# Routing attention with a PReLU layer: two pairs of batch 0 transposed by VectorE, a third pair of batch 2 in cluster order, GpSimd's transfers without pace tokens

## The chip, the cores and the metric

The kernel runs on one core of one Trainium2 chip. The time is device microseconds (us) of that core, the median of several runs of the whole kernel. The profile comes from one further execution. A core has five engines, each with its own instruction queue that is worked off in order: TensorE (PE; its weight loads are PEld), VectorE (DVE), ScalarE (ACT), GpSimd (POOL) and SyncE (SP), which here only issues transfers (DMA). Engines wait for each other through semaphores.

## The reference, cut to what matters

```python
# batch 4, heads 8, tokens 768, head size 64, clusters 16
q_assign = argmax(q_n @ c_n.T);  k_assign = argmax(k_n @ c_n.T)   # per token and head
mask   = q_assign[:, :, :, None] == k_assign[:, :, None, :]
scores = where(mask, scale * q @ k.T, -1e9)
attn   = softmax(scores);  attn_out = attn @ v
x = attn_out.transpose(0, 2, 1, 3).reshape(3072, 512)
h = x @ w_in                                      # 512 -> 2048
out = (maximum(h, 0) + alpha * minimum(h, 0)) @ w_out   # 2048 -> 512
```

A query attends only to keys of its own cluster. The weights come in 64-bit floats and are converted on the chip; everything is computed in 32-bit floats.

## The kernel before, in words

**Units of work.** Two heads make a pair; batch b has pairs 4b to 4b+3 (`pairs`, 16 in all). A step is two of the six key chunks of a pair. An ordinary pair is done in two halves of 384 queries, each in three steps: scores (`score`, L781), exponential on ScalarE (L802), masking by cluster on VectorE (`mask`, L822), sums of the rows (L832, L870, L878), weighing of v (`weigh`, L936) and normalisation into xT (`normalise`, L1039). PSUM has one tile for the weighed values (`vps`), so the next pair's weighing waits for the normalisation of the one before. In batch 0 the mask is added to the scores by a matmul (L790) of cluster memberships (`member`, `outside`, `aq`), and sums are taken by a matmul with ones (L929).

**Pairs in cluster order.** From pair `NO` = 10 on (the last two pairs of batch 2, all of batch 3) tokens are first sorted by cluster: GpSimd scatters q, k and v rows to DRAM (`order_scatter`, L673; twelve rows of tiles to each head, staged by SyncE in `order_stage`, L659), and the sorted pair is loaded again (`order_load`). A key chunk then needs only a window of 224, 320 or 384 queries, not all 768 (`window`, `weigh_near`, L969), and the pair takes three steps rather than six. Its result is turned to rows by TensorE (`to_rows`, L999), scattered back by GpSimd (`put_back`, L1008), fetched by SyncE and turned by VectorE (`fetch_back`, `turn_back`, L1027).

**The order.** `steps` lists the steps: batch 0 and 1 have 24 each, then batch 2's cluster-ordered pairs come before its ordinary ones, then batch 3; `NS` = 78. The order of the instructions on each engine is written out by hand: load and preparation pieces are hung on a step and a slot (`load_at`, `prep_at`), others come due a number of slots later (`later`, `tick`). Matmuls of the layer (`ffn_pieces`: 28 pieces to a half batch, L1063 and L1081) fill the slots evenly from one entry of `begun_at` to the next; `kept` says how many are left for the block after. The very last half batches use a scheme with fewer products (`last_pieces`).

**The first half of batch 0** (steps 0 to 11) also converts weights. SyncE loads a raw tile of 512 KB (L247; five tiles in rotation), VectorE splits it (L253, L255), ScalarE scales, VectorE joins (L265, L268), GpSimd multiplies (L271). The number of conversions begun in steps 0 to 11 is 2, 0, 2, 2, 0, 2 and then one each. All of it stands at fixed places in VectorE's queue. Batch 0's pairs are loaded in one transfer a tile (`load`, L119); TensorE transposes them by an identity (`prep_features`, L354, three groups of eight matmuls a pair) and ScalarE copies them out (L358). For later batches the load places 32x32 blocks (L127), and VectorE transposes (`prep_blocks`, L364).

**Pace.** `pace` has ScalarE write a token (L649) and GpSimd copy it (L650), so that GpSimd's next transfer waits until ScalarE has come to that slot.

**Semaphores of transfers.** Transfers of SyncE and ScalarE share eight completion semaphores in the program's order; a transfer waits until the one that used its semaphore before has landed.

Of the kernel before, what the change touches and what calls it, by code (L numbers as in the profile page):

```python
# [10 lines left out]
FP32 = mybir.dt.float32  # L11
# [3 lines left out]
I32 = mybir.dt.int32  # L15
# [8 lines left out]
def kernel(  # L24
# [77 lines left out]


    pairs = [(b, hp) for b in range(B) for hp in range(NCH)]
    NO = WHOLE * NCH - 2
    NP = len(pairs)
    raw_qk, vts = {}, {}

    Q = 32

    def load(n):

        b, hp = pairs[n]
        for w, src in enumerate((q, k)):
            raw = inp.tile([P, 2, NJ, D], FP32, name="qk")
            if n < NCH:
                nc.sync.dma_start(  # L119
                    out=raw.rearrange("p h j d -> p h (j d)"),  # L120
                    in_=src[b, 2 * hp:2 * hp + 2].rearrange("h (p j) d -> p h (j d)",
                                                            j=NJ))
            for h in range(2):
                rows = src[b, 2 * hp + h]
                for x in range(D // Q if n >= NCH else 0):
                    r = h * D + x * Q
                    nc.sync.dma_start(  # L127
                        out=raw.rearrange("p h j d -> p (h j d)")[r:r + Q, :].rearrange(
                            "p (t i) -> p t i", i=Q),
                        in_=rows[:, x * Q:(x + 1) * Q].rearrange("(t p) i -> p t i", p=Q))  # L130
            raw_qk[n, w] = raw
# [192 lines left out]
    lowest = const.tile([P, B], FP32, name="lowest")  # L324
    highest = const.tile([P, B], FP32, name="highest")
    WORDS = [float((127 + e) * 2 ** 23) for e in (-50, 40)]
    kept_of = [0]

    def inverse(n, half):

        if pairs[n][0] > kept_of[0]:
            check_inverses()
        return inverses[:, (2 * n + half) % (2 * NCH), :]

    def check_inverses():
# [156 lines left out]
    def second_part():  # L492

        first_part.close()
        for name, bufs in (("emore", 1), ("ordc", 1), ("ordp", 1), ("order", NP - NO),
                           ("xmore", 1), ("byrow", 1), ("pace", 8)):
            sorts[name] = fast.enter_context(tc.tile_pool(name=name, bufs=bufs))
        for i in range(5):
            e_tiles.insert(0, sorts["emore"].tile([P, 2, HS], FP32, name=f"more{i}"))

    def order_constants():
# [21 lines left out]
        same = brief[:, 2 * P:3 * P]  # L523
        before, within = rows[1], rows[2]
        shift = ordc.tile([P, 2], FP32, name="shift")
        sorts["paced"] = ordc.tile([1, 1], FP32, name="paced")

        def columns():
            nc.vector.tensor_reduce(out=cols, in_=own, axis=AX.X, op=ALU.add)
# [113 lines left out]
            nc.vector.tensor_reduce(out=first, in_=begunT, axis=AX.X, op=ALU.add)  # L643
        firsts[n] = first

    def pace():

        token = sorts["pace"].tile([1, 1], FP32, name="pace")
        nc.scalar.copy(token, ones[0:1, 0:1])  # L649
        nc.gpsimd.tensor_copy(out=sorts["paced"], in_=token)  # L650

    def order_stage(n, i):

        b, hp = pairs[n]
# [24 lines left out]
    def order_load(n):  # L679
        assert len(scattered[n]) == 2 * NX  # L680
        whole = scratch.pop(n)[0]
        found = sorts["order"].tile([P, 2, NJ, 1], I32, name="found")
        for h in range(2):
            r0 = 2 * h * S
            nc.sync.dma_start(out=found[:, h], in_=whole.bitcast(I32)[
                r0:r0 + S, D:D + 1].rearrange("(j p) d -> p j d", p=P))
        orders[n] = found
        for w in range(2):
            raw = inp.tile([P, 2, NJ, D], FP32, name="qk")
            for h in range(2):  # L690
                r0 = (2 * h + w) * S
                for x in range(D // Q):
                    r = h * D + x * Q
                    nc.sync.dma_start(
                        out=raw.rearrange("p h j d -> p (h j d)")[r:r + Q, :].rearrange(
                            "p (t i) -> p t i", i=Q),
                        in_=whole[r0:r0 + S, x * Q:(x + 1) * Q].rearrange(
                            "(t p) i -> p t i", p=Q))
            raw_qk[n, w] = raw
        vt = vpool.tile([P, 2, NJ, D], FP32, name="vt")  # L700
        for h in range(2):
            r0 = (2 * h + 1) * S
            nc.sync.dma_start(out=vt[:, h], in_=whole[r0:r0 + S, D:2 * D].rearrange(
                "(j p) d -> p j d", p=P))
        vts[n] = vt
# [20 lines left out]
    for b in range(B):  # L726
        whole = [n for n in range(b * NCH, (b + 1) * NCH) if n >= NO]
        rest = [n for n in range(b * NCH, (b + 1) * NCH) if n < NO]
        begun_at.append(len(steps))
        steps += [(n, None, s) for n in whole for s in range(SB)]  # L730
        for half in range(2) if rest else ():
            if half:
                begun_at.append(len(steps))
            steps += [(n, half, s) for n in rest for s in range(SB)]
            feeds[len(steps)] = b, half
    begun_at.append(len(steps))
    assert NJ == 6 and GROUP == 2

# [265 lines left out]

    def put_back(to, place, rows, i):
        j, h = divmod(i, 2)
        pace()
        nc.gpsimd.indirect_dma_start(  # L1008
            out=to[i],
            out_offset=bass.IndirectOffsetOnAxis(ap=place[:, h, j:j + 1], axis=0),  # L1010
            in_=rows[j // HJ][:, j % HJ, h * D:(h + 1) * D], in_offset=None, element_offset=h * S * D)

    def fetch_back(n, whole):
# [11 lines left out]
        def turn_back():  # L1025
            for half in range(2):
                nc.vector.transpose(out=x_tile(b, half)[:, hp, :],  # L1027
                                    in_=raw[:, half * HS:(half + 1) * HS])
        later(4 if n == NP - 1 else 9, turn_back)

    def x_tile(b, half):
        if (b, half) not in xTs:
# [106 lines left out]
    def last_pieces():  # L1139
# [93 lines left out]
        def hidden(x):  # L1233
# [33 lines left out]

            def p3():
                plus(g_of(f1, 1), product("e", "S4", x_of(1, 1), False))
                slopes(f1)  # L1270

            def p7():
                plus(g_of(f2, 1), product("a", "S3", x_of(1, 0), False))
                late.append(p4)
                if x % 2 == 0 and x:
                    g_sums(x - 2)
# [86 lines left out]
    FREE = SLOTS * SB - 3  # L1363


    ORDERS = [26, 29, 35, 38, 41, 50]
    prep_at, load_at = {}, {}
    for (n, half), u in start_of.items():
        def at(step, slot, piece):
            prep_at.setdefault((step, slot), []).append(piece)  # L1370
        if half is None:
            t = ORDERS[n - NO]
            load_at.setdefault(t, []).append(lambda n=n: load(n))
            for i in range(2):
                at(t + 1, FIRST + i, lambda n=n, i=i: order_features(n, i))
            at(t + 2, 2, lambda n=n: order_sims(n))
            load_at.setdefault(u - (3 if n == NO + 1 else 4), []).append(
                lambda n=n: order_load(n))
            at(u - 4, 0, lambda n=n: prep_clusters(n))
            for i in range(2):  # L1380
# [3 lines left out]
        if half == 0:  # L1384
# [5 lines left out]
            else:  # L1390
                load_at.setdefault(u - 9, []).append(lambda n=n: load(n))
                load_at.setdefault(u - 7, []).append(lambda n=n: load_v(n))
            if n < NCH:
                for g in range(len(groups)):
                    at(u - 4, FIRST + g, lambda n=n, g=g: prep_features(n, g))
            else:
                for w in range(2):
                    at(u - 7, FIRST + w, lambda n=n, w=w: prep_blocks(n, w))
            at(u - (3 if n < NCH else 5 if u - 6 < TOGETHER else 6), FIRST,
               lambda n=n: prep_sims(n))  # L1400
            if n >= NCH:
                at(u - 4, FIRST if u - 4 < TOGETHER else 0, lambda n=n: prep_clusters(n))
        if n < NCH:
# [19 lines left out]
    def feed_block(u):  # L1423
        if u == NS:
# [2 lines left out]
                ffn[i] = lambda piece=ffn[i], p=p: (piece(), w_in_sums(p))  # L1427
            ffn.extend(last_pieces())
            return
        ffn.extend(ffn_pieces(*feeds[u]))  # L1430

    def kept(u):


        return {NS: 12, begun_at[-2]: 8, begun_at[-3]: 2}.get(block_end(u), 0)

    def block_end(u):
        return min(x for x in begun_at if x > u)
# [59 lines left out]
    for u in range(TOGETHER, NS + 1):  # L1498
# [54 lines left out]
        for i in slots:  # L1553
# [4 lines left out]
            places = (block_end(u) - block_start(u)) // SB * FREE  # L1558
            pieces = len(ffn) - kept(u) + -whole * (places - 1 - at_slot) // places
            todo.popleft()()  # L1560
            room = 0 if steps[u - SB][1] is None else 1 + (s == 0)
            if room and sorting:
                pace()
            while sorting and room:
                scatters, piece = sorting.popleft()
                piece()
# [229 lines left out]
```

## Time and profile before

| | |
|---|---|
| median of 3 runs | 945.04 us (944.75 to 946.84) |
| the profiled execution | 944.23 us, span 942.5 us |
| TensorE clock granted | 0.999 |
| busy: PE, PEld | 924.1, 496.5 us |
| busy: DVE, ACT, POOL | 663.5, 265.9, 351.2 us |
| chain that ended last | PE 87%, DVE 6%, SP's queue 2%, DMA 2% |
| transfers of SP and ACT | 60.35 MB in 201840 packets on the large queue |

Batch 0's first half runs from 13.5 to about 74 us, its second half to 196, batch 1 to 445, batch 2 to 644, batch 3 to about 750, and the last half batches of the layer to the end. A group in the profile is given as line, engine, operation, tile written <- tiles read, size and count, then busy time and mean duration in ns of one record, then the idle time of the engine just before them and what ended it. A float32 matmul leaves two records. Busy time of overlapping records counts once.

### The profile page before, as it was taken

The numbers are of one execution on the slowest core, as the hardware profiler recorded it, in microseconds if no ns is written. First come the engines' busy times: TensorE is split into PE (matmuls) and PEld (weight loads), VectorE is DVE, ScalarE is ACT, GpSimd is POOL, SyncE is SP. The second block draws the span as 40 slices with busy tenths as digits, with TensorE's granted clock in tenths as the row PEclk, the third lists the DMA queues.
The fourth block names the chain that finished last, engine by engine and source line by source line (L and its number), as shares of the span: only waits on it lengthen the run. The fifth ranks groups of instructions, "written<-read, shape, count | busy, mean of one in ns | idle before, by whom it ended". The sixth has DMA issues, their size and how long they took to land.

```text
span 942.5 us, 11891 instructions
## 1 busy us (share of the span) xinstructions
PE 924.1 (98%) x3995; PEld 496.5 (53%) x3995; DVE 663.5 (70%) x1247; ACT 265.9 (28%) x658; POOL 351.2 (37%) x529
## 2 busy tenths in 40 slices
PE   8999999999999999999999999999999999999997
PEld 5534444445455454454544545545455555556886
DVE  5797788799679589698995955456888535698100
ACT  5764444323123032331322322223133121221000
POOL 2333222200016576467534686364256670000000
PEclk9999999999999999999999999999999999999999
DMA  8333658039001645165920134333441112000000
GB/s 297 125 127 96 146 130 149 18 59 198 1 6 53 159 87 133 47 120 131 155 52 12 43 80 101 63 67 62 93 75 34 32 37 53 1 0 1 23 23 26
DMA packets 209668, 73.38 MB, mean 78 GB/s; under 512 B 194288, under 2 KB 198080, under 8 KB 209600
## 3 DMA queue, kind: packets, MB, share of 16 engines
q1 hardware_dynamic: 201840, 60.35, 29.2%
q0 software_dynamic: 6912, 11.81, 4.1%
q8 instruction: 33, 0.54, 0.2%
q10 hardware_dynamic: 848, 0.39, 0.2%
q14 instruction: 35, 0.29, 0.1%
HBM read 49.89 MB, written 22.28 MB: 77 GB/s over the span
## 4 chain that ended last, share of the span: by engine, by line
PE 87%; DVE 6%; SPq 2%; DMA 2%; issue 1%; POOL 1%; ACT 1%; ACTq 0%; DVEq 0%; POOLq 0%
PE fps L1081 26%; PE fps L1063 25%; PE vps L936 7%; PE sps L781 7%; PE sps L1297 4%; PE sps L1241 4%; PE fps L781 2%; PE vps L1297 2%; PE vps L1241 2%; PE fps L1297 1%; PE fps L1241 1%; PE sps L790 1%; PE vps L969 1%; PE mps L969 1%; PE mps L381 1%
## 5 line engine op out<-in xcount | busy, mean ns | idle before, releaser
L1063 PE MATMUL fps<-xT,w_in_sb 128*128 128x384 f32 x768 | 257.7, 490 | 0.0
L1081 PE MATMUL fps<-w_out_sb,gT 128*128 128x512 f32 x576 | 254.4, 595 | 1.1 <-DVE gT L1055 1.1
L1063 PEld LDWEIGHTS fps<-xT,w_in_sb 128*128 128x128 f32 x768 | 142.8, 190 | 102.6 <-issue 3.8
L1081 PEld LDWEIGHTS fps<-w_out_sb,gT 128*128 128x128 f32 x576 | 107.5, 190 | 133.4 <-issue 123.0
L673 POOL DMA_INDIRECT scratch<-stage,off x144 | 155.4, 1079 | 49.7 <-issue 25.1
L650 POOL COPY paced<-pace 1x1 f32<-1x1 f32 x196 | 55.5, 283 | 202.3 <-ACT pace L649 201.5
L1069 ACT COPY gT<-fps 128x384 f32<-128x384 f32 x96 | 46.0, 479 | 215.6 <-PE fps L1063 215.6
L1055 DVE SCALAR_TENSOR_TENSOR gT<-gT,alpha 128x384 f32<-128x384 f32 x96 | 61.3, 648 | 50.4 <-ACT gT L1069 50.3
L781 PE MATMUL sps<-qkT 64*128 64x384 f32 (+1 forms) x480 | 88.6, 487 | 0.0
L1008 POOL DMA_INDIRECT back<-rows,found x72 | 74.9, 1040 | 18.2 <-issue 16.1
L802 ACT ACTIVATE E<-sps 128x768 f32<-128x768 f32 (+1 forms) x78 | 57.9, 790 | 59.4 <-PE sps L790 38.8
L781 PEld LDWEIGHTS sps<-qkT 64*128 64x128 f32 x480 | 42.7, 186 | 40.5 <-issue 15.0
L822 DVE SCALAR_TENSOR_TENSOR more<-aq,key,more 128x384 f32<-128x384 bf16 (+2 forms) x120 | 63.0, 584 | 1.2 <-ACT more L799 1.1
L936 PE MATMUL vps<-E,vt 128*64 128x384 f32 x316 | 58.6, 495 | 1.4 <-DVE xT L1039 1.4
L904 DVE RECIPROCAL inverses<-mps 64x12 f32<-64x12 f32 (+1 forms) x44 | 10.9, 248 | 58.5 <-PE mps L891 58.1
L822 DVE SCALAR_TENSOR_TENSOR E<-aq,key,E 128x384 f32<-128x384 bf16 (+2 forms) x96 | 50.2, 577 | 1.9 <-ACT E L799 1.8
L271 POOL TENSOR_TENSOR w_in_sb<-w_in_sb,power 128x512 f32<-128x512 f32 x16 | 25.1, 1573 | 67.8 <-DVE w_in_sb L268 67.8
L832 DVE TENSOR_TENSOR acc<-acc,E 128x768 f32<-128x768 f32 x37 | 35.3, 953 | 14.7 <-ACT E L802 13.6
L271 POOL TENSOR_TENSOR w_out_sb<-w_out_sb,power 128x512 f32<-128x512 f32 x16 | 22.9, 1434 | 57.3 <-DVE w_out_sb L268 57.3
L802 ACT ACTIVATE more<-sps 128x768 f32<-128x768 f32 (+1 forms) x42 | 31.1, 775 | 33.1 <-PE sps L781 32.0
L1087 ACT COPY y<-fps 128x512 f32<-128x512 f32 x18 | 10.6, 586 | 99.1 <-PE fps L1081 99.1
L1089 DVE TENSOR_TENSOR y<-y,fps 128x512 f32<-128x512 f32 x24 | 16.4, 683 | 29.1 <-PE fps L1081 29.1
(283 smaller groups left out, 1167.2 us busy)
## 6 DMA issues: line engine op xcount, KB each, us to landing
raw<-in_moe_w_in_dram SPq DMA_DIRECT2D x16, 512.0 KB
raw<-in_moe_w_out_dram SPq DMA_DIRECT2D x16, 512.0 KB
out_dram<-y SPq DMA_DIRECT2D x21, 256.0 KB
qk<-in_q_dram SPq DMA_DIRECT2D x48, 96.0 KB
qk<-in_k_dram SPq DMA_DIRECT2D x48, 96.0 KB
qk<-scratch SPq DMA_DIRECT2D x48, 96.0 KB
w_in_kept<-w_in_sb SPq DMA_DIRECT2D x8, 512.0 KB
vt<-in_v_dram SPq DMA_DIRECT2D x10, 384.0 KB
```

The lines of the kernel that those rows point to most:

```text
L650: nc.gpsimd.tensor_copy(out=sorts["paced"], in_=token)
L673: nc.gpsimd.indirect_dma_start(out=scratch[n][1][h * NX + xx], out_offset=bass.IndirectOffsetOnAxis(ap=ranks[n][:, xx, h:h + 1], axis=0), ...
L781: nc.tensor.matmul(out=bank(ps, h, m), lhsT=qkT[r:r + D, S + c * P:S + (c + 1) * P], rhs=qkT[r:r + D, tokens], start=True, stop=not early_ ...
L802: nc.scalar.activation(out=E[:, :, 0:m], in_=ps[:, :, 0:m], func=AF.Exp, scale=SCALE)
L822: nc.vector.scalar_tensor_tensor(out=e, in0=of, scalar=keys[n][:, NJ + c, h:h + 1], in1=e, op0=ALU.is_equal, op1=ALU.mult)
L936: nc.tensor.matmul(out=po[r:r + D, 0:HS], lhsT=vts[n][:, h, c, :], rhs=e[:, h, :], start=(c == 0), stop=(c == NJ - 1))
L1008: nc.gpsimd.indirect_dma_start(out=to[i], out_offset=bass.IndirectOffsetOnAxis(ap=place[:, h, j:j + 1], axis=0), in_=rows[j // HJ][:, j % ...
L1055: nc.vector.scalar_tensor_tensor(out=gs[f], in0=gs[f], scalar=alpha[:, f:f + 1], in1=gs[f], op0=ALU.mult, op1=ALU.max)
L1063: nc.tensor.matmul(out=ps[:, 0:HS], lhsT=w_in_sb[:, c, f * P:(f + 1) * P], rhs=xTs[b, half][:, c, :], start=(c == 0), stop=(c == NCH - 1))
L1081: nc.tensor.matmul(out=ps[:, 0:DM], lhsT=gs[f][:, i * P:(i + 1) * P], rhs=w_out_sb[:, f, :], start=on and f == f0, stop=off and f == f0 + ...
L1241: nc.tensor.matmul(out=bank[to], lhsT=w_in_form(m, x, cc), rhs=rhs[:, cc, :], start=start and cc == 0, stop=cc == KH - 1, skip_group_check ...
L1297: nc.tensor.matmul(out=bank[to], lhsT=g_form(m, x, t), rhs=w_out_form(n, x), start=start and x == 0, stop=x == NQ - 1, skip_group_check=no ...
```

## The change

- `NB0` = 2: pairs 2 and 3 of batch 0 are loaded in 32x32 blocks, in 16 transfers for each tile instead of one (two heads, two halves of the columns, four groups of tokens), and VectorE transposes them (`prep_blocks`, at step u-4) in place of TensorE and ScalarE.
- `NO` goes from 10 to 9: pair 9, the second of batch 2, is done in cluster order too. The places where orders begin (`ORDERS`) and where sorted pairs are loaded are adapted. Batch 2's one ordinary pair no longer starts a block of the layer between its halves: batch 1's last half fills batch 2's 15 steps, and both halves of batch 2 fill batch 3's 12 steps. `NS` becomes 75.
- `pace` and its tiles are gone; the numbers of scattered pieces in a slot are no longer zero after a cluster-ordered pair.
- Moved: the check of the inverses (three slots after the last of a batch, not before the first of the next), `turn_back` (seven slots, not nine), `prep_sims` of one ordinary pair (one slot later), `slopes(f1)` in the last part (two pieces later).
- The rows' numbers read back in `order_load` go into the tile of the ranks, not one of their own.

```diff
-    NO = WHOLE * NCH - 2
+    NO = WHOLE * NCH - 3
+    NB0 = 2
     def load(n):
         b, hp = pairs[n]
         for w, src in enumerate((q, k)):
             raw = inp.tile([P, 2, NJ, D], FP32, name="qk")
-            if n < NCH:
+            if n < NB0:
                 nc.sync.dma_start(
...
+            for h in range(2 if NB0 <= n < NCH else 0):
+                rows = src[b, 2 * hp + h].rearrange("(g p j) d -> g p j d", p=Q, j=NJ)
+                for x in range(D // Q):
+                    r = h * D + x * Q
+                    to = raw.rearrange("p h j d -> p (h j d)")[r:r + Q, :].rearrange(
+                        "p (j g i) -> p g j i", g=P // Q, i=Q)
+                    for g in range(P // Q):
+                        nc.sync.dma_start(out=to[:, g], in_=rows[g][:, :, x * Q:(x + 1) * Q])
...
-        if pairs[n][0] > kept_of[0]:
-            check_inverses()
+        b = pairs[n][0]
+        inverted[b] += 1
+        if inverted[b] == 2 * NCH and b < B - 1:
+            later(3, check_inverses)
...
-    def pace():
-        token = sorts["pace"].tile([1, 1], FP32, name="pace")
-        nc.scalar.copy(token, ones[0:1, 0:1])
-        nc.gpsimd.tensor_copy(out=sorts["paced"], in_=token)
...
-        found = sorts["order"].tile([P, 2, NJ, 1], I32, name="found")
+        found = ranks[n].rearrange("p x h -> p (x h)")[:, 0:2 * NJ].rearrange(
+            "p (h j d) -> p h j d", h=2, d=1)
...
-            if half:
+            if half and not whole:
                 begun_at.append(len(steps))
             steps += [(n, half, s) for n in rest for s in range(SB)]
-            feeds[len(steps)] = b, half
+            feeds[len(steps)] = [(b, 0), (b, 1)] if whole else [(b, half)]
...
         j, h = divmod(i, 2)
-        pace()
         nc.gpsimd.indirect_dma_start(
...
-        later(4 if n == NP - 1 else 9, turn_back)
+        later(4 if n == NP - 1 else 7, turn_back)
...
                 plus(g_of(f1, 1), product("e", "S4", x_of(1, 1), False))
-                slopes(f1)
...
                 plus(g_of(f2, 1), product("a", "S3", x_of(1, 0), False))
+                slopes(f1)
...
-    ORDERS = [26, 29, 35, 38, 41, 50]
+    ORDERS = [26, 29, 35, 38, 41, 53, 56]
...
-            load_at.setdefault(u - (3 if n == NO + 1 else 4), []).append(
+            load_at.setdefault(u - (3 if n in (NO + 1, NO + 2, NP - 1) else 4), []).append(
...
-            if n < NCH:
+            if n < NB0:
                 for g in range(len(groups)):
                     at(u - 4, FIRST + g, lambda n=n, g=g: prep_features(n, g))
             else:
                 for w in range(2):
-                    at(u - 7, FIRST + w, lambda n=n, w=w: prep_blocks(n, w))
+                    at(u - (4 if n < NCH else 7), FIRST + w,
+                       lambda n=n, w=w: prep_blocks(n, w))
...
-               lambda n=n: prep_sims(n))
+               lambda n=n: prep_sims(n)) if u - 6 < 2 * TOGETHER else at(
+                   u - 6, FIRST + 1, lambda n=n: prep_sims(n))
...
-        ffn.extend(ffn_pieces(*feeds[u]))
+        for b, half in feeds[u]:
+            ffn.extend(ffn_pieces(b, half))
...
-        return {NS: 12, begun_at[-2]: 8, begun_at[-3]: 2}.get(block_end(u), 0)
+        return {NS: 12, begun_at[-2]: 2, begun_at[-3]: 2}.get(block_end(u), 0)
...
-            room = 0 if steps[u - SB][1] is None else 1 + (s == 0)
-            if room and sorting:
-                pace()
+            room = 1 + (s == 0 or (u >= NS - 30 and (s, i) == (1, 0)))
```

## The prediction

> **What bounds the kernel now.** I read the engines' shares first, then busy time by stage, then the timelines of the two stages that the change touches, then the instruction groups for prices.
>
> ```profile
> PE 924.1 (98%) x3995; PEld 496.5 (53%) x3995; DVE 663.5 (70%) x1247; ACT 265.9 (28%) x658; POOL 351.2 (37%) x529
> ```
>
> TensorE's records cover 98% of the 942.5 us, so a gain must take TensorE work away, and a loss must open a gap in it. By stage (us, then busy time of PE, PEld, DVE, ACT, POOL; clock; DMA share):
>
> ```profile
> 34.00:72.50 38.50, 35.60 (x338) 15.98 (x340) 36.68 (x71) 25.98 (x41) 13.94 (x9) 1.00 0.40 125
> 445.50:562.20 116.70, 113.02 (x473) 58.53 (x472) 92.65 (x175) 32.43 (x105) 63.64 (x100) 1.00 0.36 67
> ```
>
> The first row is most of batch 0's first half: VectorE is busy 36.7 of 38.5 us, more than TensorE. There two engines are full, and VectorE sets the pace. The second row is the first block of batch 2. Timelines of batch 0 (start, duration; in brackets the idle time before and what ended it):
>
> ```profile
> 45.42 1.09 PE L354 MATMUL fps<-ident,qk 128*64 128x128 f32 x16 [1.48 <-ACT qkT L358]
> ...
> 68.02 0.54 PE L936 MATMUL vps<-E,vt 128*64 128x384 f32 x2 [1.42 <-DVE xT L1039]
> ```
> ```profile
> 31.74 0.38 DVE L942 STREAM_TRANSPOSE simT<-fps 128x192 f32<-128x192 f32 x1 [3.35 <-PE fps L929]
> ...
> 40.38 0.39 DVE L253 TENSOR_SCALAR power<-raw 128x512 uint32<-128x512 uint32 x1
> ...
> 67.41 0.56 DVE L1039 TENSOR_TENSOR xT<-vps,rd 128x384 f32<-128x384 f32 x1
> ```
>
> After 31.74 VectorE has no wait until 72.9, and at 68.02 TensorE waits for VectorE's normalisation of pair 2. So what VectorE does between 31.7 and 67.4 sets when TensorE may start pair 3. SyncE's queue in that stage:
>
> ```profile
> 6.85 0.38 SPq L119 DMA_DIRECT2D qk<-in_q_dram  x1
> 8.54 0.37 SPq L119 DMA_DIRECT2D qk<-in_k_dram  x1
> ...
> 12.29 0.38 SPq L119 DMA_DIRECT2D qk<-in_q_dram  x1
> 13.64 0.38 SPq L119 DMA_DIRECT2D qk<-in_k_dram  x1
> 23.54 1.55 SPq L247 DMA_DIRECT2D raw<-in_moe_w_out_dram  x2
> ...
> 36.52 0.33 SPq L247 DMA_DIRECT2D raw<-in_moe_w_out_dram  x1
> ```
>
> The four L119 transfers load pairs 2 and 3. The queue then stands waiting for free weight buffers: the weights (L247) are early.
>
> [...] So an instruction that waits holds all behind it in SP's queue. The trace agrees: by its semaphore updates the raw tile issued at 9.48 landed at 19.75, and each transfer re-using one of the eight completion semaphores was issued only after that one's landing. [...] The trace shows neighbours spaced by their durations plus 0.05 us. [...]
>
> **The change part by part.**
>
> *Pairs 2 and 3 of batch 0, TensorE and ScalarE.* Removed: 48 matmuls (L354), two bursts seen at 25.76 to 28.52 and 42.02 to 46.45, that is 2.8 and 2.9 us of work plus the 1.48 us gap: 7.2 us of TensorE's time there. Six ScalarE copies (0.59 us each) go too, off the path. Added on VectorE: four transposes of 128x768 at 0.95 us (row L364, 947 ns), 1.9 us before step 3 and 1.9 us before step 6. Cover of the first is the 3.35 us idle time above, shrunk by 2.8 us; the second has none. Were this all, VectorE would reach pair 2's normalisation about 0.5 us later than now, and the 7.2 us would be spent waiting for it: cost about zero.
>
> *The same pairs, SP's queue.* Each tile is now loaded by 16 transfers (two heads, two halves of the columns, four groups): 64 in place of 4, at steps 0 and 2, ahead of vt2, raw3 and raw4 (first) and of the next raw tiles and vt3 (second). Their price p is not in the trace; nearest are transfers of small blocks on the same queue:
>
> ```profile
> L659 SPq DMA_DIRECT2D stage<-in_q_dram x36: 595/596/827, 228.3 to 656.2; - x36
> L659 SPq DMA_DIRECT2D stage<-in_k_dram x36: 595/615/959, 229.0 to 656.8; - x36
> ```
>
> With the gap between neighbours that is 0.65 us. L127 (four times as many rows each) has medians of 536 and 568 ns, thus 0.57 to 0.6; the lowest issue of any kind is 0.30. I bound p by 0.35 and 0.75 and take 0.65: like the L659 ones and the small ones on ScalarE's queue (L474, median 600 ns) the new ones gather rows with strides on both sides. Walk: the eighth new transfer cannot go before 13.8, since its semaphore belongs to vt1, which lands at 13.81 by the updates. Then 24 more x 0.65 = 15.6: pair 2 is issued at 29.4. vt2, raw3, raw4 (1.5): 31. Pair 3: 32 x 0.65 = 20.8, to about 52. Only then the fifth weight conversion's raw tile (now issued at 23.54) goes out, at 52; the one issued alone at 36.52 landed 3.6 us later, so it lands at about 55.8. VectorE's split of this tile (L253, at 40.38 now) stands in program order before everything of steps 4 to 12. VectorE waits for it, and so do pair 1's and pair 2's normalisations behind it, and TensorE behind these. Lateness: 55.8 - 40.4 = 15.4, plus 1.9 for pair 3's transposes: 17.3 us at pair 2's normalisation, about 85 instead of 68. As a formula: 56p - 19. ScalarE's aq transfers (L474) share the eight semaphores and are held too (pair 2's to about 53, now 41.3), inside the same delay. Of the 17.3 about 0.5 comes back in VectorE's next wait for TensorE (76.45). After 75 TensorE is busy 123.9 of 125 us, so the rest stays. Sum of batch 0: **+16.8 us**.
>
> *Pair 9 (batch 2, second pair) in cluster order.* Records are two to a matmul.
>
> ```profile
> L781 PE MATMUL sps<-qkT 64*128 64x384 f32 x432 | 83.4, 500 | 0.0
> L936 PE MATMUL vps<-E,vt 128*64 128x384 f32 x316 | 58.6, 495 | 1.4 <-DVE xT L1039 1.4
> ```
>
> Scores: 48 records x 0.193 = 9.3 us become 24 of 384, 320 and 224 columns (eight each x 0.20, 0.19, 0.15) = 4.3: -5.0. Weighing: 48 x 0.185 = 8.9 become 4.0 (L969's groups add up to 24 for six pairs): -4.9. Added: return to rows (L999) 5.9/6 = 1.0, begins (L599) 3.5/6 = 0.6; sums saved 0.35; similarities (L573 for L381) equal. Net **-8.6 us** of TensorE.
>
> *What comes with it.* Steps 78 to 75; batch 1's last FFN half now fills 15 steps rather than 12, batch 2's two halves the next 12. Adding the changed program's instructions of those 15 steps at their rows' prices (VectorE's scaled by 663.5/731, the busy time over the sum of durations) gives TensorE 131 us and VectorE 125; now the block has 115 and 94. VectorE is at 95% there, and pair 8's first half alone wants 30 us of it against 26 of TensorE. Nothing that I can name hides that: I put **+4 us** of gaps, between 0 and 10. The next block is full of TensorE work (46 pieces), VectorE 90 us: no gap.
>
> *Pace tokens.* Gone: 196 ScalarE copies of 0.18 us and 196 GpSimd copies of 0.28. GpSimd's transfers (about 1.05 us each, 252 instead of 216) then run as soon as data is there. The waits for them sit on GpSimd, not on TensorE: 0. Were they to crowd the loads, the DMA share of 0.3 to 0.5 leaves room; I bound it by -2 and +3. *The moved waits* (inverses' check, turning back two slots earlier, one similarity step by a slot, slopes by two pieces): each moves one or a few VectorE instructions past others; the waits they could touch are 0.9 to 1.4 us singly. Order numbers kept in the rank tile: no cost. Together 0, within 2.
>
> Sum on the profiled execution: 944.2 + 16.8 - 8.6 + 4 = 956.4. It lies 0.8 below the median of 945.04; I give 956.5.
>
> **Rivals.**
> *A, as summed*: 950 to 962. For it: the order of the queue and the price of L659.
> *B, short issues*: if p is at most 0.375 the raw tile lands by 40.4 and batch 0 costs 0.5 us; 944.2 + 0.5 - 8.6 + 4 = 940, faster. The change gains over all when 56p - 19 is under 4.6, that is p under 0.42. Against it: no burst of block loads in this trace is under 0.5 us an issue; for it: single issues of 0.30 to 0.38.
> *C, VectorE's block*: as A, and block 48 to 62 is bound by VectorE with gaps of 10 us or more, or landings slower among the small packets: 963 to 970.
> *D, part of the price*: p of 0.45 to 0.55, lateness 6 to 12: 945 to 950.
>
> **How the numbers follow.** A 0.62, C 0.12, D 0.12, B 0.14. The range of 941 to 966 takes in A, D, most of C and the edge of B. A difference under about 0.2% (1.9 us) can't be told from none: faster 0.14, same 0.05 (D's low end), slower 0.81.
>
> **What would show it.** In the changed profile SP's queue should be full of the new line's issues from 7 to about 52 us, 0.6 us each; VectorE should show one idle stretch of some 10 us before a split of a raw tile near 55; TensorE's gaps before 75 us should sum to over 15 us, and pair 2's normalisation end near 85. L781 and L936 should lose about 10 us, and the end of the weights' loads come later by the same 17. I am wrong if the issues take under 0.42 us, or if VectorE's split doesn't wait.

## The result, and the profile after

The changed kernel takes 977.38 us (976.21 to 978.38) beside 944.98 for the kernel before: a ratio of 1.0338, interval 1.0320 to 1.0356. The direction was as forecast, the size was not: 32.4 us against 11.5, and outside the range of 941 to 966. The profiled execution took 977.64 us with a span of 975.9 (before: 942.5), so 33.4 us are to be found in it. In what follows an execution over 1.5% above the fastest of the same kernel counts as slow; e3, e4, r1 and e10 have such ones, so their spread stands beside their medians (r1's ratio leaves the slow one out).

The page first: the share of the engines, and the digits of TensorE's granted clock.

```profile
PE 925.1 (95%) x3867; PEld 494.4 (51%) x3867; DVE 661.0 (68%) x1250; ACT 242.4 (25%) x450; POOL 327.5 (34%) x375
...
PEclk9869999999999999999998899999999999999999
```

The forecast took 5.7 us of work (batch 0; 7.2 with a gap) and 8.6 us (pair 9) from TensorE, yet its busy time rose by 1.0. The clock digits show one reason: there are slices below 9, which the kernel before did not have. The clock records show half clock in six periods, 45.4 us in all (before, one of 4.7 us after the last matmul). Five of them begin in or just after a gap in TensorE's work, the sixth after its last matmul. TensorE's records inside them cover 22.0 us; taken as work at twice its time (an estimate from the granted 0.5; eight matmuls of L940 take 2.83 us there and 1.51 at full clock, 1.9 times as long), that is 11 us of extra busy time, and without it the work is about 10 us less than before, not the 14.3 of the forecast. The time not covered by TensorE's records grew by 32.4 us.

By stage (us, then busy time of PE, PEld, DVE, ACT, POOL; clock; DMA share): batch 0 from step 4 to step 12, and batch 2's first block, 15 steps now.

```profile
39.40:96.70 57.30, 38.80 (x300) 15.17 (x296) 42.12 (x82) 25.22 (x40) 13.98 (x10) 0.82 0.43 128
462.90:610.30 147.40, 133.64 (x567) 68.95 (x566) 121.21 (x232) 33.52 (x69) 88.46 (x93) 0.95 0.53 98
```

In the first row VectorE, which was busy 36.7 of 38.5 us before, stands for 15 of 57. In the second it is busy 121 of 147 us, 82%: so it is not full there, contrary to my forecast.

Batch 0 in three timelines (start, duration, in brackets the idle time before and what ended it). SyncE's queue:

```profile
8.24 13.33 SPq L130 DMA_DIRECT2D qk<-in_q_dram  x16
21.67 11.12 SPq L130 DMA_DIRECT2D qk<-in_k_dram  x16
...
34.52 11.60 SPq L130 DMA_DIRECT2D qk<-in_q_dram  x16
46.22 10.63 SPq L130 DMA_DIRECT2D qk<-in_k_dram  x16
56.95 1.01 SPq L255 DMA_DIRECT2D raw<-in_moe_w_out_dram  x2
```

VectorE:

```profile
61.03 0.43 DVE L261 TENSOR_SCALAR power<-raw 128x512 uint32<-128x512 uint32 x1 [13.42 <-DMA raw<-in_moe_w_out_dram]
...
89.05 0.56 DVE L1042 TENSOR_TENSOR xT<-vps,rd 128x384 f32<-128x384 f32 x1
```

TensorE, with the largest gap of batch 2 as well:

```profile
33.28 0.47 PE L794 MATMUL sps<-aq,outside 32*128 32x384 bf16 x1 [4.83 <-DMA aq<-member]
...
63.48 2.93 PE L785 MATMUL sps<-qkT 64*128 64x384 f32 x8 [15.75 <-ACT E L806]
...
89.67 0.91 PE L940 MATMUL vps<-E,vt 128*64 128x384 f32 x2 [1.71 <-DVE xT L1042]
...
534.62 1.71 PE L582 MATMUL mps<-qk,cT 128*32 128x384 f32 x8 [8.76 <-ACT rows L1006]
```

ScalarE in batch 0:

```profile
31.05 1.37 ACTq L484 DMA_DIRECT2D aq<-member  x2
...
61.49 0.72 ACT L267 ACTIVATE power<-power,low_exp 128x512 uint32<-128x512 uint32 x1 [17.40 <-DVE power L261]
```

The queue is full of the new line's issues from 8.2 to 56.9 us, the raw tile behind them goes out at 56.95, VectorE stands 13.4 us for it, and pair 2's normalisation comes at 89.05 instead of 67.41. Step 12, which began at 73.6 us, begins at 96.7: +23.1. The 15.75 us gap is named "ACT E": ScalarE's exponentials stood behind its scaling of the same raw tile (L267), which waited 17.4 us for VectorE's split. The 4.83 us gap came another way: ScalarE's aq transfer of 31.05 uses a completion semaphore that one of pair 2's transfers, landed at 31.03, had before it. Batch 0 so holds 23 of the 33 us.

The other 10 us open in batch 2. TensorE before, where it has no wait at pair 10's features, then ScalarE and GpSimd after:

```profile
489.51 0.85 PE L573 MATMUL mps<-qk,cT 128*32 128x384 f32 x8
```
```profile
534.09 0.48 ACT L1006 COPY rows<-mps 128x384 f32<-128x384 f32 x1 [11.22 <-DMA back<-rows,off]
```
```profile
482.22 0.98 POOL L676 DMA_INDIRECT scratch<-stage,off  x1 [32.45 <-DMA stage<-in_v_dram]
...
514.82 0.96 POOL L676 DMA_INDIRECT scratch<-stage,off  x1 [0.30 <-DMA stage<-in_k_dram]
516.08 0.96 POOL L1011 DMA_INDIRECT back<-rows,off  x1 [0.30 <-ACT E L806]
517.03 0.21 POOL L673 COPY stage<-number 64x4 int32<-64x4 int32 x1
```

GpSimd stood 32 us for a stage load (which stood in SP's queue behind a store of y and the loads that follow it), then had a row of scatters (L676) to do before pair 9's first put-back (L1011) at 516. Put-backs and scatters then take turns. ScalarE cannot copy pair 10's rows until pair 9's have left the only two row buffers: it waits 11.2 us, and TensorE, which needs the PSUM tile that this copy reads, 8.8. One of the groups that lost work to pair 9, two records to a matmul (busy us, mean ns of one, idle before):

```profile
L940 PE MATMUL vps<-E,vt 128*64 128x384 f32 x292 | 56.7, 514 | 1.7 <-DVE xT L1042 1.7
```

It has 24 records fewer than before (316), but the mean of one has risen from 495 to 514 ns: the half clock, spread over the group.

### The profile page after: what moved, and what is told of

Same layout as the page of the kernel before. It is cut to its first block, busy times and chain, and to the rows that moved or that the text cites. A ratio compares the mean times of both kernels' runs of the same rounds, so it can differ in the third digit from the quotient of the medians.

```text
span 975.9 us, 11316 instructions
## 1 busy us (share of the span) xinstructions
PE 925.1 (95%) x3867; PEld 494.4 (51%) x3867; DVE 661.0 (68%) x1250; ACT 242.4 (25%) x450; POOL 327.5 (34%) x375
## 3 DMA queue, kind: packets, MB, share of 16 engines
q1 hardware_dynamic: 229952, 62.73, 30.3%
## 4 chain that ended last, share of the span: by engine, by line
PE 75%; DVE 7%; DMA 7%; SPq 4%; POOL 3%; issue 3%; ACT 0%; ACTq 0%; DVEq 0%; POOLq 0%
PE fps L1066 21%; PE fps L1084 21%; PE sps L785 6%; PE vps L940 5%; PE sps L1244 4%; PE sps L1300 4%; SPq L130 3%; PE vps L1300 2%; PE vps L1244 2%; PE fps L785 2%; POOL scratch L676 2%; POOL back L1011 1%; DMA scratch<-stage,off 1%; DMA vt<-in_v_dram 1%; DMA raw<-in_moe_w_out_dram 1%
## 5 line engine op out<-in xcount | busy, mean ns | idle before, releaser
L676 POOL DMA_INDIRECT scratch<-stage,off x168 | 176.2, 1049 | 199.9 <-DVE acc L836 66.5
L1011 POOL DMA_INDIRECT back<-rows,off x84 | 86.3, 1028 | 98.7 <-ACT rows L1006 60.4
L826 DVE SCALAR_TENSOR_TENSOR more<-aq,key,more 128x384 f32<-128x384 bf16 (+2 forms) x116 | 60.5, 579 | 0.1
L940 PE MATMUL vps<-E,vt 128*64 128x384 f32 x292 | 56.7, 514 | 1.7 <-DVE xT L1042 1.7
L279 POOL TENSOR_TENSOR w_in_sb<-w_in_sb,power 128x512 f32<-128x512 f32 x16 | 22.4, 1403 | 91.3 <-DVE w_in_sb L276 91.3
L826 DVE SCALAR_TENSOR_TENSOR E<-aq,key,E 128x384 f32<-128x384 bf16 (+2 forms) x88 | 45.3, 569 | 0.6 <-ACT E L803 0.6
L836 DVE TENSOR_TENSOR acc<-acc,E 128x768 f32<-128x768 f32 x35 | 33.3, 952 | 14.6 <-ACT E L806 13.6
L279 POOL TENSOR_TENSOR w_out_sb<-w_out_sb,power 128x512 f32<-128x512 f32 x16 | 22.8, 1423 | 59.8 <-DVE w_out_sb L276 59.8
L940 PEld LDWEIGHTS vps<-E,vt 128*64 128x64 f32 x292 | 19.2, 142 | 27.6 <-issue 24.5
```

The costliest lines, as they stand in the source:

```text
L676: nc.gpsimd.indirect_dma_start(out=scratch[n][1][h * NX + xx], out_offset=bass.IndirectOffsetOnAxis(ap=ranks[n][:, xx, h:h + 1], axis=0), ...
L826: nc.vector.scalar_tensor_tensor(out=e, in0=of, scalar=keys[n][:, NJ + c, h:h + 1], in1=e, op0=ALU.is_equal, op1=ALU.mult)
L940: nc.tensor.matmul(out=po[r:r + D, 0:HS], lhsT=vts[n][:, h, c, :], rhs=e[:, h, :], start=(c == 0), stop=(c == NJ - 1))
L1011: nc.gpsimd.indirect_dma_start(out=to[i], out_offset=bass.IndirectOffsetOnAxis(ap=place[:, h, j:j + 1], axis=0), in_=rows[j // HJ][:, j % ...
```

## The experiments

All times are medians beside runs of the kernel before on the same chip, which stayed between 944.7 and 945.6 us on every chip. The chips matter here, so they are named A (first four runs), B, C and D. The chip of the runs in the section above is not on record.

| kernel | chip | us | ratio to before, interval |
|---|---|---|---|
| e1: batch 0 as before | A | 955.10 | 1.0112 (1.0095 to 1.0129) |
| e2: batch 0's part alone | A | 963.71 | 1.0211 (1.0181 to 1.0240) |
| e5: four transfers a tile | A | 954.13 | 1.0104 (1.0085 to 1.0123) |
| e8: pair 3 through GpSimd | A | 965.79 | 1.0218 (1.0201 to 1.0235) |
| e3: before, no tokens | B | 997.84 (980.33 to 1008.10) | none given |
| e3b: and scatters beside put-backs | B | 1014.27 | 1.0760 (1.0714 to 1.0807) |
| e4: e1, second rows | B | 1041.29 (1030.17 to 1054.59) | 1.1020 (1.0940 to 1.1100) |
| e6: e1, tokens back | B | 986.41 | 1.0436 (1.0419 to 1.0454) |
| r1: e1 again | C | 1014.88 (1009.66 to 1030.91) | 1.0715 (1.0667 to 1.0762) |
| r3: e3 again | C | 998.34 | 1.0532 (1.0448 to 1.0616) |
| r0: the changed kernel again | C | 1046.91 | 1.1089 (1.1051 to 1.1126) |
| r4: e4 again | C | 1038.23 | 1.1032 (1.0923 to 1.1141) |
| e7: e6, scatters kept apart | D | 967.25 | 1.0226 (1.0161 to 1.0291) |
| e9: before, spaced, no tokens | D | 953.25 | 1.0075 (1.0057 to 1.0093) |
| e10: e7 without tokens | D | 989.67 (966.78 to 1002.57) | none given |
| r5: e3 again | D | 971.24 | one run |
| e11: e7, longer ring | B | 974.26 | 1.0302 (1.0279 to 1.0325) |
| e12: e11's order, spaced | B | 950.58 | 1.0057 (1.0037 to 1.0076) |

### e1 and e2: the two halves of the loss

```diff
 e1 (changed kernel)         e2 (kernel before)
-    NB0 = 2                 +    NB0 = 2, load by 16 transfers for NB0 <= n < NCH,
+    NB0 = NCH               +    prep_blocks at u - 4 for those pairs
```

> The changed kernel with pairs 2 and 3 of batch 0 loaded and turned as before (NB0 = 4); all the rest of the change stays. Theory (SP's queue costs batch 0 its 23 us, the rest of the change 10 us): 954 to 957. Rival (the loss comes mostly from pair 9 in cluster order and the missing pace): above 968. My prediction's own sum for this kernel was 945.0 - 8.6 + 4 = 940.4.

> The kernel before with only the batch 0 part of the change (pairs 2 and 3 loaded by 16 transfers a tile, turned by VectorE). Theory: 945 + 23 = 966 to 970, the two parts of the change add up. My prediction's sum for this part was +16.8, so 961.8. Rival (the two parts make each other worse): below 960.

Measured: e1 955.10, e2 963.71. Batch 0's part costs 18.4 us alone and 977.38 - 955.10 = 22.3 within the change (the 977 is from other runs than e1's); the rest costs 9.8. The two halves add up to 28.2, 4.2 us short of the whole. In e1 the gap of batch 2 stands where it stood, as TensorE's timeline shows:

```profile
511.39 1.71 PE L582 MATMUL mps<-qk,cT 128*32 128x384 f32 x8 [8.87 <-ACT rows L1006]
```

TensorE's busy time in e1 is 922.8 us, 1.3 less than before, with 13.6 us of half clock before the last microseconds of the kernel. TensorE's records cover 9.6 us of these, so by the same estimate, work at twice its time, 4.8 us of the busy time are the clock's; without them the work is 6.1 us less. That is 2.5 short of pair 9's forecast gain of 8.6. The profiled execution is 10.8 us longer than before: 6.1 less work, 4.8 more for the clock, and 12.1 more without a record of TensorE's, of which the gap above is 8.87.

### e5 and e8: what in batch 0 costs the time

```diff
 e5: -            for h in range(2 if NB0 <= n < NCH else 0): ... 16 transfers a tile
     -                for x in range(D // Q if n >= NCH else 0):
     +                for x in range(D // Q if n >= NB0 else 0):
 e8: -                        nc.sync.dma_start(out=to[:, g], ...)
     +                        (nc.sync if n == 2 else nc.gpsimd).dma_start(out=to[:, g], ...)
```

> The changed kernel with pairs 2 and 3 of batch 0 loaded by 4 transfers a tile instead of 16, in the layout of the later batches; VectorE still turns them. Their queries and keys then stand in another order than their values, so the rows of batch 0 are not the reference's; sizes and instructions are unchanged otherwise. Theory (the number of issues in SP's queue is the cost): 953 to 958, as without the batch 0 part. Rival (VectorE's four more transposes or its place in the program cost the time): above 968.

> The changed kernel with the 32 new transfers of pair 3 issued by GpSimd; pair 2's 32 stay on SP's queue. All transfers stay as small as they are. Theory (issues in SP's queue): SP's queue is free near 31, the fifth raw tile lands near 36 in place of 61, and batch 0 costs at most 6 us: 954 to 962. Rival (the small packets land slowly or crowd the weights, whoever issues them): above 968.

e5 leaves batch 0's rows in another order, but moves the same data. It takes 954.13 us: with 16 issues instead of 64 the raw tile goes out at 29.75, and batch 0's part costs nothing (nor does it gain: 1 us below e1).

```profile
29.75 0.94 SPq L246 DMA_DIRECT2D raw<-in_moe_w_out_dram  x2
```

Its rows are as short as the change's (128 bytes; 229184 packets on the large queue, 229952 in the change), so it is not small packets that cost. VectorE's four extra transposes add nothing to the time there, and the time in SP's queue is the cost. e8 takes 965.79, between what the two theories expected. SP's queue was free at 33, as expected, but the issues then stood in GpSimd's, ahead of the weights' last step (L279). GpSimd's and VectorE's timelines of e8:

```profile
27.84 9.20 POOL L130 DMA_DIRECT2D qk<-in_q_dram  x16
...
50.79 1.27 POOL L279 TENSOR_TENSOR w_in_sb<-w_in_sb,power 128x512 f32<-128x512 f32 x1
```
```profile
52.10 0.43 DVE L261 TENSOR_SCALAR power<-raw 128x512 uint32<-128x512 uint32 x1 [4.15 <-POOL w_in_sb L279]
```

An issue on GpSimd takes 0.56 us, nearly as long as on SyncE (0.60). Moving the issues moved the wait: the weights' chain passes through both queues.

### e3, e3b, e4, e6: the tokens, and a surprise

```diff
 e3:  -                pace()          (both calls; kernel before)
 e3b: e3, and
      -            room = 0 if steps[u - SB][1] is None else 1 + (s == 0)
      +            room = 1 + (s == 0 or (u >= NS - 30 and (s, i) == (1, 0)))
 e4:  e1, and  rows = outT's own halves for pairs 10, 12, 14; turn_back of pairs 9 and 10 after 14 slots
 e6:  e1, and  + pace()  at every scatter and put-back, as in the kernel before
```

> The kernel before with the pace tokens gone and nothing else: the 196 ScalarE copies, the 196 GpSimd copies and the waits of GpSimd for them. The prediction's term was 0 (-2 to +3), so 945 with 943 to 948. Rival (the tokens keep transfers from colliding): above 950.

> The kernel before with the tokens gone and scatters also handed out in the steps in which rows are put back (the new rule for room). Theory (scatters ahead of the put-backs in GpSimd's queue are a cause of batch 2's loss): 947 to 955, with the put-backs late in the stage after 490. Rival (that rule is harmless, only pair 9 in cluster order makes the loss): 943 to 947.

> The changed kernel with batch 0 as before; pair 10's rows are put back from its own output tile instead of the single pair of row buffers, and pairs 9 and 10 are turned back 14 slots after the fetch instead of 7. The transfers and their order on GpSimd are unchanged. Theory (late put-backs reach TensorE only through the row buffers and the early turning back): the gap of 8.9 us at 502 and the one after it go, 940 to 946. Rival (VectorE is too full in that block, my +4 of 0 to 10): 950 to 956.

> The changed kernel with batch 0 as before and the pace tokens put back, at every scatter and put-back, with the new rule for room. Theory (order in GpSimd's queue, not its speed, makes the put-backs late): no gain, 953 to 960. Rival (without the tokens the scatters ran ahead and crowded the rest out): 940 to 948.

All four lie far above every expectation but e3's rival. e3 takes only tiny copies and the waits for them away, and its four executions lose 35 to 63 us; the profile is of the fastest. VectorE, ScalarE, TensorE and GpSimd of e3 around 300 us, in this order:

```profile
311.89 0.56 DVE L1038 TENSOR_TENSOR xT<-vps,rd 128x384 f32<-128x384 f32 x1 [15.51 <-issue]
```
```profile
313.31 0.49 ACT L799 ACTIVATE more<-fps 128x384 f32<-128x384 f32 x1 [21.64 <-remote]
```
```profile
313.86 4.56 PE L1062 MATMUL fps<-xT,w_in_sb 128*128 128x384 f32 x8 [16.73 <-issue]
```
```profile
295.79 0.98 POOL L673 DMA_INDIRECT scratch<-stage,off  x1 [0.43 <-issue]
297.07 0.95 POOL L673 DMA_INDIRECT scratch<-stage,off  x1 [0.30 <-issue]
298.33 0.96 POOL L673 DMA_INDIRECT scratch<-stage,off  x1 [0.30 <-issue]
...
310.92 0.96 POOL L673 DMA_INDIRECT scratch<-stage,off  x1 [0.31 <-issue]
```

TensorE, VectorE and ScalarE stand together for 15 us, "issue" and "remote": nothing that the records show ends the wait. By their operands VectorE (L1038) and ScalarE (L799) wait for TensorE's semaphore, and the matmuls that raise it have their records at 294 to 296; the two go on at 311.9 and 313.3. When the semaphore rose can't be read: of the events that the semaphores of TensorE, VectorE and ScalarE should leave between 289 and 297 us, the trace has 7 of 20, while the kernel before has all 22. The DMA semaphores have events throughout. GpSimd meanwhile issues one indirect transfer after another, 1.26 us apart, and SyncE goes on too. I call this a stop. e3's profile has 16 us of stops, e3b 28, e4 47, e6 14, counted where all three engines stand for over 1 us. Half clock and catching up follow (17.1 us of half clock after e3's long stop), so the loss is larger than the sum. The kernel before, on the same chip, is unharmed at 944.9.

### The same kernels on another chip

> The changed kernel with batch 0 as before, once more, beside e3's and e4's kernels on one chip. In e3, e4 and e6 there are stretches of 2 to 17 us in which TensorE, VectorE and ScalarE stand together while GpSimd issues transfers; in the first run of this kernel there is none. Theory 1 (such stops come with the unpaced transfers and differ from chip to chip): on a chip where e3's kernel takes over 975 this one takes over 965 too; on a chip where it takes 955 e3's kernel takes at most 955. Theory 2 (they belong to the kernel's own order): 953 to 957 again, beside e3's kernel over 975.

> The kernel before without the tokens, once more. Theory 1 (chip): near 945 to 955 on a chip without stops, 980 to 1010 with them. Theory 2 (the kernel's own order): 980 to 1010 again, whatever the chip.

> The changed kernel itself on the same chip. Theory 1: 976 to 979 on a chip without stops, over 985 on one with them. Theory 2: 976 to 979.

> The kernel of e4 on the same chip. Theory 1: without stops 940 to 948 (the late put-backs then no longer reach TensorE), with them above 1000. Theory 2: 1030 to 1055 again.

The edits are those of e1, e3, none, and e4. On chip C e1's kernel takes 1014.88 us, 60 more than on A, and the changed kernel itself 1046.91, 70 more than on record. Theory 1 holds: without the tokens the time depends on the chip. (e3's kernel was not run on A; that it loses nothing there is not shown. A, C and D were each used on one occasion, so something else that differed between the occasions is not ruled out.) The page of the changed kernel on C:

```profile
PE 942.3 (90%) x3867; PEld 501.6 (48%) x3867; DVE 661.4 (63%) x1250; ACT 242.7 (23%) x450; POOL 320.9 (31%) x375
```

The stops have a pattern. In all nine profiles of kernels without tokens on chips B, C and D the first stop begins 18.4 to 19.0 us into the first unbroken series of transfers, after 13 or 14 of them. It is each time the same first series of the program, so whether the number of transfers or the place in the program counts is not told apart. On chip A and in the first profile of the changed kernel it passes without a stop; so does a series of 48, less than 3 us apart, in e8. r4 answers e4's question in part: r1 has a wait of 13.15 us for "ACT rows" at 552 us, r4 on the same chip has at most 0.95, and where pair 10's copy goes to another tile one of 5.76 us, which holds a stop of 4.1. This fits the row buffers as the path by which late put-backs reach TensorE, but the stops hide what that is worth.

### e9 to e12: what the tokens do, and whether a version wins

```diff
 e9:  kernel before; in pace():
      -        nc.scalar.copy(token, ones[0:1, 0:1])
      -        nc.gpsimd.tensor_copy(out=sorts["paced"], in_=token)
      +        for _ in range(3):
      +            nc.gpsimd.memset(sorts["paced"], 0.0)      (1 x 80; before every transfer)
 e7:  e6, and
      +            if steps[u - SB][1] is None and steps[u][0] < NO + 3:
      +                room = 1 - i % 2
      +            else:
      +                room = 3 if s == 0 else 1 + (i == 2) + ((s, i) == (2, 0))
 e10: e7 without pace()
 e11: e7, ("pace", 16) for ("pace", 8); order_load of pairs 10 and 11 at u - 4
 e12: e11 with two memsets (1 x 64) before every transfer in place of the tokens
```

> The kernel before with each token replaced by three short GpSimd memsets (about 0.5 us together), one group before every transfer: the transfers are spaced in time, but wait for nobody. Theory A (transfers issued back to back stop the engines): as before, 944 to 950, on any chip. Theory B (they must be held to ScalarE's progress, since they run ahead): 970 to 1010 on a chip with stops.

> The kernel of e7 without the tokens. On a chip with stops: theory (stops come with unpaced transfers) over 965; on a chip without: 936 to 945. Rival (the order of scatters and put-backs is all): 936 to 945 on any chip.

> The changed kernel with batch 0 as before, the pace tokens back, and at most one scatter in two slots while rows are put back (more per slot elsewhere). Theory (stops need unpaced transfers, and batch 2's loss needs scatters ahead of the put-backs): no stop of all engines over 3 us, no TensorE gap over 3 us in batch 2, 936 to 943. Rival (pair 9's VectorE work costs what its TensorE work saves, my +4 of 0 to 10): 945 to 952.

> The kernel before without the tokens, one look, to tell what chip this is: 980 to 1010 with stops, 944 to 955 without.

r5 shows that chip D has stops (971.24, one of 9.1 us). e9, on the same chip, has none between 250 and 800 us and takes 953.25. GpSimd in e9:

```profile
287.69 0.58 POOL L649 MEMSET paced<- 1x80 f32 x3
288.44 0.97 POOL L673 DMA_INDIRECT scratch<-stage,off  x1 [0.17 <-issue]
289.41 0.58 POOL L649 MEMSET paced<- 1x80 f32 x3
```

Nothing is waited for; the transfers are 1.7 us or more apart instead of 1.26. Time between them is enough here, without holding them to ScalarE. e9 is still 7.6 us slower than the kernel before. One part is that the memsets also delay the put-backs: VectorE waits 10.8 us for the last ones, and TensorE has a gap of 3.2 us behind it at 795. In e10 the wait for rows has shrunk to almost nothing, while stops take the time:

```profile
532.47 1.06 PE L583 MATMUL mps<-qk,cT 128*32 128x384 f32 x8 [0.61 <-ACT rows L1013]
```

So the gap of 8.8 us goes when scatters no longer stand ahead of the put-backs. e7, with order and tokens, should have won and takes 967.25. Its stops are 3.2 us at most and 6.7 in all, so they are only a part of its 21.6 us. ScalarE and VectorE of e7:

```profile
478.88 0.19 ACT L659 COPY pace<-ones 1x1 f32<-1x1 f32 x1 [11.73 <-POOL paced L660]
```
```profile
466.35 0.98 DVE L721 STREAM_TRANSPOSE qkT<-qk 128x768 f32<-128x768 f32 x1 [7.02 <-DMA qk<-scratch]
```

The tokens pass through a ring of eight buffers, so when GpSimd stands for a stage load, ScalarE stands for GpSimd; and pair 10's load left SP's queue late. That these two are what e7 lost is argued from the lines.

> The kernel of e7 with 16 token buffers instead of 8, and pairs 10 and 11 loaded four steps ahead instead of three. Theory (the ring and the late load are what is left of batch 2's loss): 938 to 948. Rival (three near pairs leave GpSimd and SP too little time in batch 2): 955 to 970.

> The kernel of e11 with two short GpSimd memsets (about 0.35 us together) ahead of every transfer in place of the tokens; ScalarE is not involved. Theory (spacing in time keeps the stops away, and ScalarE's ring was a cost): 938 to 948, no stop of all engines over 3 us. Rival (such short spacing is not enough): stops, over 955.

e11 is no better (974.26): its largest gap, 12.55 us, holds a stop of 8.5 us at 607, after a row of 31 transfers since 559.7 us, nearly all with their tokens ready, the last ones 1.3 us apart. Tokens space the transfers only while GpSimd is ahead of them. The stop also hides whether the longer ring and the earlier load gained anything. e12 takes 950.58 on chip B, where e1's relatives take 974 to 1041: no stop above 1.6 us, one gap left.

```profile
509.98 1.71 PE L583 MATMUL mps<-qk,cT 128*32 128x384 f32 x8 [6.54 <-ACT rows L1013]
```

With the memsets GpSimd is again late with the put-backs, also in this order. No version beat the kernel before; e12 comes within 5.7 us of it.

## Why the prediction was wrong

*What bounds the kernel, and the way in batch 0*: right. VectorE's split of the sixth raw tile (the prediction counts from nought and says fifth) was the place, SP's queue the cause (e5), and by e5 no other part of batch 0 cost anything. *The price p* of 0.65 us: measured 0.60 us and 0.05 between neighbours. The new issues began at 8.24, not in a stream from 6.85, and the first 16 took 0.83 each, as some waited for their semaphores; so the raw tile left at 56.95 instead of 52 and the split came 5.2 us later than forecast.

*Batch 0's sum of +16.8*: e2 measures 18.4 alone, 22.3 within the change. The term was near alone and 5.5 us too small within it, and the mis-sized part is the start and the semaphore waits of the first issues. Step 12 begins 23.1 us late: 20.7 at the split (15.4 forecast), 1.0 more on VectorE to pair 2's normalisation (1.9 forecast), and 1.5 for which the forecast had no term, TensorE's half clock after it. In e2 the issues begin at 6.84 and the split comes at 59.35.

*The half clock*: TensorE's clock falls to 0.5 within the gaps of 4.83, 15.75 and 8.76 us, 2.9, 4.1 and 3.8 us after they begin, and stays there for 6.8, 17.1 and 10.2 us. Periods of 3.4 us, of which these lengths are whole multiples, also come with gaps of 1.71 and 2.94 us; the kernel before has gaps of up to 1.58 us and no such period before its last matmul has ended. So a gap can cost more than its length: the eight matmuls of L940 behind the 1.71 us gap take 1.3 us longer than at full clock. What sets the start and the length of a period is not shown.

*Pair 9, -8.6*: right in direction as TensorE's work, but 2.5 us too large (6.1 by e1's account), and wrong as time.

*VectorE's block, +4*: the step failed. It put the loss on VectorE at 95%, and VectorE is at 82%. In its place e1 measures +9.8 for the rest of the change where -4.6 was forecast, 14.4 us more (15.4 by the profiled executions). By e1's account the 15.4 are 2.5 us of work not saved, 4.8 of half clock and 8.1 of gaps beyond the 4. The largest gap, 8.87 us, is put-backs standing behind scatters on GpSimd, by the timelines and by e10, where it is gone. The missing tokens, the new rule for scatters in a slot and the third pair in cluster order can all bring scatters in front of the put-backs, and no run on a chip without stops separates them. I had counted three near pairs' instructions for TensorE and VectorE, and not for GpSimd, which now has 36 put-backs instead of 24 and scatters in the same steps.

*Pace, 0 (-2 to +3)*: wrong on chips B, C and D, not tried alone on A. I costed the tokens by the copies that they are, and said that GpSimd's waits are on no one's path. In the first runs of the changed kernel and in e1 no stop shows, so stops are not what made the 32.4 us. But on chips B, C and D taking the tokens away costs 26 to 54 us by itself (r5, e3, r3), and the changed kernel 102 us in all on C. The cover that I named, room in the DMA share, was not what counted.

*The moved waits, 0*: in e1, which has them, step 24 begins at 196.4 us, 196.6 before, so in batch 0 they cost nothing; those of batches 2 and 3 were not tried alone. *The rivals*: C came nearest in number, and gaps of about 10 us came in its block, but not from VectorE; slower landings were no large part (the late raw tile was split 4.1 us after its issue, 3.8 in the sum). B and D fell with the price.

*The sum*: 16.8 - 8.6 + 4 is 12.2, which beside the median makes 957.2; the 956.5 takes the 0.8 between median and profile the wrong way. The walk to the raw tile adds up to 55.3, not 55.8. Neither changes the outcome. Of the 32.4 us, 5.5 beyond the forecast are batch 0's and 14.4 the rest's: 12.2 + 5.5 + 14.4 = 32.1.

## What to carry over

Count every queue that a change loads with the same care as the busy engine: an instruction that issues a transfer mostly took its queue 0.3 to 0.6 us here, and all that stands behind it is late by the sum (the raw tile went out at 56.95 instead of 23.54). A wait that looks idle may be what keeps two things apart; before it is taken out, ask what runs back to back without it, and time the result on more than one chip. Where one engine's order mixes early work with urgent work, put the urgent first, or the slack of one becomes the gap of the other.

## What was not expected of the hardware

During GpSimd's indirect transfers, 1.26 us apart, TensorE, VectorE and ScalarE can stand together for up to 17 us, first after 13 or 14 transfers (18.4 to 19.0 us), on three of four chips. With transfers 1.7 us or more apart (e9) they do not; 1.46 us apart (e12) the longest stop is 1.6. What holds them stays open.

One rival is the recording itself. Every execution of the experiments was recorded (each has a span and a clock), so that the stops come without it is not shown. On chips B, C and D the traces lack semaphore events: e3's has 1817 of the 1999 that TensorE, VectorE and ScalarE should leave, and the missing ones lie where GpSimd transfers, from 275 us on. e1's trace on chip A lacks none. But e9, which has no stop, lacks 96, so lost events alone are not a stop.

Fetching of instructions does not look like the cause: in e3 the trace's instruction packets lie at 276 and 326 us, none between. That the chips differ is shown by e1's kernel alone, 955.10 and 1014.88 us; why they differ was not found.
